# A gated-MLP block behind retention attention on one core: fewer tiles turned by TensorE, more by DMA, and a new order of the first loads

## The chip, the cores and the metric

The kernel runs on one core of a Trainium2 chip. The metric is the device time of one execution in microseconds (us); it was measured three times before the change: 209.21, 209.40 and 210.75 us, median 209.4 us.

## What is computed

Inputs are float32. q, k and v have 8 batches, 8 heads, 576 positions and 64 features. First comes attention with a decay instead of a softmax, then a block with a gate that mixes positions:

```python
scores = scale * np.matmul(q, k.transpose(0, 1, 3, 2))
ret = scores * Dmat          # Dmat[h, t, s] = gamma_h ** (t - s) for t >= s, else 0
x = matmul(ret, v)           # heads joined: (8, 576, 512)
h = gelu(x @ w_in)           # 512 -> 1024
u, v = h[..., :512], h[..., 512:]
v_n = (v - mean) / sqrt(var + 1e-6) * g_ln
v_s = einsum('ts,bsd->btd', w_sg, v_n) + b_sg[None, :, None]
out = x + (u * v_s) @ w_out
```

## The kernel before, in words

**Units and pairs.** The work is cut into 36 units (N). Two batches form a pair of 1152 rows; a pair has nine units (U = 9), and there are four pairs. A unit holds q, k and v of 256 positions for four heads (or, the fifth of a pair, the unit MID, the last 64 positions of both batches for all heads): three loads of 256 KB, for MID six of 128 KB in shorter rows. Two units that lie side by side together give two tiles of 128 rows of x.

**Attention, per unit i.** `load` (L311) issues the loads on SyncE's queue (SP). `scaled` (L504) multiplies q and v by powers of the decay (gq and gv) and turns q, k and v to bf16, on POOL for most units. Then q and k must be turned so that the 64 features lie on partitions, which makes qkT. For the first TD = 20 units TensorE (PE) turns them: eight transposes (L547) into PSUM and one copy by VectorE (DVE, L550). For the other 16 units `transposed` (L491) issues one DMA transpose for two units on SP (L499). `score` (L566) makes the products of q and k, `mask` (L577) applies the triangle, `states` (L596) makes the k-v products that carry the past into later units, `keep` (L626) adds them up on ScalarE (ACT) and DVE, and `outp` (L678) makes x, which ACT and DVE write to xT. From unit 9 on (JOIN = 8) outp of unit i-1, score of i and states of i are one visit of PE; before that they are three.

**The block, per tile of 128 rows.** `mlp_V` (L815) multiplies x by the second half of w_in (four matmuls of 512 columns, L821), and ACT, DVE and POOL make the normalised v_n. `mlp_U` (L857) multiplies by the first half (L868). `batch` (L878) does the mixing of positions (L890) and the product with w_out (L923); for the first 18 of 36 tiles x is added by four more PE transposes (L926), for the last 18 a DMA transpose of x (xr, L913) is added by DVE.

**What sets the order.** Every step is given to a planner (`Plan`, L120) with an engine, a cost, a key, its reads and writes. A table written out by hand (TURN, L19) gives each step its place in one sequence of some 1200 places; `emit` goes through it in that order and issues each step on its engine. An engine takes its steps strictly in that order. Where the planner's own clock shows PE idle in the first 45 us, `idle` (L147) puts in matmuls of zeros (L301) that feed nothing.

**Loads and weights.** There are six buffers for q and k (qkf) and six for v (vf). `lb` (L308) gives the first four units only two of them (0, 1, 1, 0), and unit MID waits for the load of unit 3. `w_load` (L338) brings w_in in four pieces of 512 KB on POOL's queue; the DMA itself turns float32 into bf16. Two pieces hold the second half (for mlp_V), two the first half (for mlp_U). The first is issued at 7.73 us, and the two of the first half wait for vb of unit 1. g_ln and b_sg are loaded with one number to a partition (`g_and_b`, L390), w_sg and w_out on SP (`weights`, L447).

Of the kernel before, what the change touches and what calls it, by code (L numbers as in the profile page):

```python
# [19 lines left out]
    "b_col": [57],  # L20
    "b_rows": [0, 58],
    "b_tr": [72],
    "dtab": [33],
# [4 lines left out]
    "g_col": [76],  # L28
    "g_col1": [89],
    "g_inv": [90],  # L30
    "g_rows": [21, 109],
    "g_tr": [121],
    "gelu": [51],
# [6 lines left out]
    "ident": [4],  # L40
# [12 lines left out]
    "otu": [48, 55, 92, 110, 136, 162, 197, 268, 304, 335, 377, 419, 447, 472, 498, 539, 554, 582, 610, 640, 673,  # L53
        703, 718, 751, 782, 823, 839, 883, 914, 946, 969, 1004, 1026, 1053, 1068, 1101],
    "out": [381, 477, 403, 384, 652, 668, 612, 790, 677, 777, 757, 788, 760, 880, 906, 932, 1069, 1070, 979, 1074,
        1082, 1132, 1135, 1115, 1105, 1094, 1124, 1144, 1150, 1146, 1158, 1174, 1178, 1184, 1183, 1188, 1190],
    "qkT": [32, 16, 44, 95, 111, 137, 170, 203, 263, 296, 334, 360, 401, 413, 421, 465, 514, 533, 550, 581, 588, 641,
        715, 754, 855, 893, 965, 1052],
    "qs": [22, 9, 40, 45, 102, 125, 154, 168, 246, 261, 267, 309, 350, 354, 386, 404, 436, 437, 487, 501, 516, 570,
        634, 639, 658, 653, 738, 696, 741, 833, 854, 843, 915, 917, 973, 937],  # L60
    "ret": [36, 35, 26, 27, 75, 69, 99, 101, 115, 116, 155, 148, 186, 194, 222, 226, 292, 279, 305, 332, 343, 363,
# [58 lines left out]
class Plan:  # L120
# [36 lines left out]
    def emit(self):  # L157
# [16 lines left out]
        for n in sorted(range(len(units)), key=lambda n: self.place[n]):  # L174
# [12 lines left out]
            if e == "PE" and t < FILL_END:  # L187
                self.idle(free[e], t)
# [18 lines left out]
def kernel(  # L207
# [757 lines left out]
    for i in range(N):  # L965
# [7 lines left out]
        if not i:  # L973
            for c in (0, 2):
                w_load(1, c)
# [41 lines left out]
```

## Time and profile before

| | us |
|---|---|
| median of three runs | 209.4 |
| the profiled execution, its time | 209.62 |
| its span (first to last instruction) | 207.9 |
| PE busy | 194.2 |
| DVE, POOL, ACT busy | 150.8, 135.8, 134.7 |
| the matmuls of zeros (L301), part of PE busy | 11.4 |

The sum of the lines on PE is the length of the span less the time in which PE has nothing. A line of the chain of waits has its start, its length and what ran; a line of the view by stretches has the stretch, the length, the busy time of each engine with its count of instructions, the clock that TensorE was granted (1.00 is full speed), the mean busy share of the 16 DMA engines (it can be over 1.00, since packets of one engine overlap) and the GB/s that they moved.

### The profile page before, as it was taken

What the parts mean: (1) busy time and instruction counts of PE and PEld (TensorE: products, weight loads), DVE (VectorE), ACT (ScalarE), POOL (GpSimd) and SP (SyncE); (2) the same over time, 40 slices, a digit from 0 to 9 for tenths busy, and PEclk for the clock granted to TensorE, in tenths of its full rate; (3) what the DMA queues carried; (4) which work ended last, traced back from release to release, by engine and by line L of the source; (5) the groups of instructions that cost most, each with busy time, mean ns of one, the idle gap of its engine ahead of it and who ended that gap; (6) DMA issues with size and microseconds to landing.
All of it is one profiled execution on the core that took longest, in us unless ns stands there. A gap on an engine that the chain in (4) does not pass through costs nothing.

```text
span 207.9 us, 7429 instructions
## 1 busy us (share of the span) xinstructions
PE 194.2 (93%) x2994; PEld 124.2 (60%) x3027; DVE 150.8 (73%) x366; ACT 134.7 (65%) x316; POOL 135.8 (65%) x231
## 2 busy tenths in 40 slices
PE   6977949999999999999999999999999999999992
PEld 2543536768767776567745666575656565664651
DVE  1654953998987888978786658575869689896672
ACT  5363325799999846788589776765777377826400
POOL 6557989489769996759779865749846866123200
PEclk9999966999999999999999999999999999999999
DMA  5999999999999998695999899998998999895815
GB/s 145 267 203 192 228 274 302 300 296 309 192 277 251 290 330 213 175 241 136 265 210 299 229 175 199 271 317 208 255 267 236 201 175 262 192 189 195 249 54 202
DMA packets 98321, 48.20 MB, mean 232 GB/s; under 512 B 42288, under 2 KB 92720, under 8 KB 98288
## 3 DMA queue, kind: packets, MB, share of 16 engines
q1 hardware_dynamic: 97056, 46.56, 90.0%
q0 software_dynamic: 1088, 1.05, 3.6%
q8 instruction: 23, 0.38, 0.8%
q10 hardware_dynamic: 144, 0.13, 0.2%
q14 instruction: 10, 0.08, 0.1%
HBM read 32.79 MB, written 9.44 MB: 203 GB/s over the span
## 4 chain that ended last, share of the span: by engine, by line
PE 85%; DMA 8%; POOL 2%; issue 2%; DVE 1%; SPq 0%; DVEq 0%; POOLq 0%
PE p_d L890 19%; PE p_d L868 16%; PE p_d L923 14%; PE p_d L821 14%; PE p_oz L692 7%; PE p_d L547 4%; DMA w_in<-in_moe_w_in_dram 4%; PE p_s L572 3%; DMA vf<-in_v_dram 3%; PE p_d L926 2%; DMA qkf<-in_q_dram 1%; PE p_oz L605 1%; PE p_d L301 1%; PE p_d L460 1%; POOL vb L537 1%
## 5 line engine op out<-in xcount | busy, mean ns | idle before, releaser
L586 DVE TENSOR_TENSOR ret<-p_s,tri 128x512 bf16<-128x512 f32 x64 | 42.5, 681 | 3.2 <-PE p_s L572 3.0
L537 POOL TENSOR_TENSOR vb<-vf,gv 128x512 bf16<-128x512 f32 x36 | 37.6, 1046 | 6.9 <-DMA vf<-in_v_dram 6.0
L890 PE MATMUL p_d<-wT,vn 128*128 128x288 bf16 x256 | 40.5, 286 | 0.0
L868 PE MATMUL p_d<-xT,w_in 128*128 128x512 bf16 (+2 forms) x224 | 37.9, 314 | 2.1 <-DMA w_in<-in_moe_w_in_dram 2.1
L534 POOL TENSOR_TENSOR qkb<-qkf,gq 128x512 bf16<-128x512 f32 x35 | 36.5, 1047 | 4.3 <-DMA qkf<-in_q_dram 2.8
L821 PE MATMUL p_d<-w_in,xT 128*128 128x512 bf16 x126 | 34.8, 380 | 1.3 <-issue 0.5
L923 PE MATMUL p_d<-w_out,uT 128*128 128x512 bf16 (+1 forms) x137 | 34.5, 373 | 0.9 <-issue 0.5
L898 DVE TENSOR_TENSOR uT<-p_d,uT 128x288 bf16<-128x288 f32 x64 | 27.6, 448 | 6.1 <-PE p_d L890 4.8
L890 PEld LDWEIGHTS <-vn 128*128 128x128 bf16 x256 | 24.4, 98 | 7.1
L873 ACT ACTIVATE uT<-p_d 128x512 bf16<-128x512 f32 x36 | 21.2, 596 | 11.1 <-PE p_d L868 11.0
L853 ACT ACTIVATE vn<-vg,stat 128x512 bf16<-128x512 f32 x32 | 25.6, 814 | 3.8 <-POOL stat L840 3.7
L868 PEld LDWEIGHTS <-w_in 128*128 128x128 bf16 x224 | 19.4, 101 | 13.6 <-DMA w_in<-in_moe_w_in_dram 2.3
L838 POOL TENSOR_TENSOR stat<-stat,mhalf 128x1 f32<-128x1 f32 x36 | 20.2, 562 | 11.0 <-DVE stat L832 6.0
L824 ACT ACTIVATE vg<-p_d 128x512 f32<-128x512 f32 x36 | 20.9, 596 | 9.3 <-PE p_d L821 9.2
L829 DVE BATCH_NORM_STATS2 stat<-vg 128x6 f32<-128x512 f32 x36 | 24.6, 684 | 2.5 <-ACT vg L824 2.4
L530 POOL CAST qkb<-qkf 128x512 bf16<-128x512 f32 x32 | 19.5, 613 | 8.5 <-DMA qkf<-in_k_dram 5.8
L550 DVE COPY qkT<-p_d 128x1024 bf16<-128x1024 bf16 x20 | 13.7, 683 | 11.7 <-PE p_d L547 11.5
L923 PEld LDWEIGHTS <-uT 128*128 128x128 bf16 x148 | 13.7, 98 | 13.1
L821 PEld LDWEIGHTS <-xT 128*128 128x128 bf16 x144 | 13.0, 98 | 12.2 <-DVE xT L772 0.4
L837 POOL TENSOR_SCALAR stat<-stat 128x1 f32<-128x1 f32 x26 | 5.6, 217 | 20.7 <-DVE stat L830 15.6
L890 PE MATMUL p_d<-wT,vmid 128*128 128x288 bf16 x64 | 18.4, 287 | 0.0
L547 PE MATMUL p_d<-ident,qkb 128*128 128x128 bf16 x160 | 13.3, 229 | 1.0 <-POOL qkb L534 0.8
(103 smaller groups left out, 308.3 us busy)
## 6 DMA issues: line engine op xcount, KB each, us to landing
out_dram<-ob SPq DMA_DIRECT2D x35, 256.0 KB, 3.9
qkf<-in_q_dram SPq DMA_DIRECT2D x32, 256.0 KB, 5.4
qkf<-in_k_dram SPq DMA_DIRECT2D x32, 256.0 KB, 5.5
vf<-in_v_dram SPq DMA_DIRECT2D x32, 256.0 KB, 5.6
wsg<-in_moe_w_sg_dram SPq DMA_DIRECT2D x4, 288.0 KB, 5.1
w_in<-in_moe_w_in_dram POOLq DMA_DIRECT2D x4, 256.0 KB, 5.7
qkf<-in_k_dram SPq DMA_DIRECT2D x8, 128.0 KB, 5.1
qkf<-in_q_dram SPq DMA_DIRECT2D x8, 128.0 KB, 5.0
```

The costliest lines, as they stand in the source:

```text
L534: plan.add("POOL" if i else "DVE", 1010 if i else 700, key, lambda: eng.tensor_tensor(split(qs[a]), shape(qkf[l][:, 0, :]), gain(gq), op=A ...
L537: plan.add("POOL", 1010, key + 2, lambda: nc.gpsimd.tensor_tensor(shape(vb[a][:]), shape(vf[l][:]), gain(gv), op=Alu.mult), reads=rd(i, 2) ...
L547: nc.tensor.transpose(banks[0][:].bitcast(BF)[:, (x * KK + kk) * 128:(x * KK + kk + 1) * 128], src[:, kk * 128:(kk + 1) * 128], ident[:])
L586: nc.vector.tensor_tensor(ret[r][x][:].rearrange("p (s k j) -> p s k j", s=2, k=2), banks[0][:].rearrange("p (s k) j -> p s k j", s=2), tr ...
L821: nc.tensor.matmul(banks[0][:], xT[p % NX][:, m, kk, :], w_in[:, kk, F2:], start=(kk == 0), stop=(kk == KK - 1))
L829: nc.vector.bn_stats(st[:, 0:6], vg[g][:])
L853: nc.scalar.activation(vn[p % 2][m][:], vg[g][:], Act.Identity, scale=st[:, 8:9], bias=st[:, 9:10])
L868: nc.tensor.matmul(hu[:, c, :].rearrange("p (t j) -> p t j", j=128), w_in[:, kk, 128 * (x * per + c):128 * (x * per + c) + 128], xT[p % NX ...
L873: plan.add("ACT", 500, key, lambda banks, x=x: nc.scalar.activation(uT[p % NX][:, x * per:x * per + per, cols], banks[0][:].rearrange("p ( ...
L890: nc.tensor.matmul(banks[0][:, :HS], src[:, 128 * c:128 * c + 128], wT[e][j][:, half * HS:(half + 1) * HS], start=(j == 0), stop=(j == SB ...
L898: plan.add("DVE", 380, key, lambda banks, c=c, col=col: nc.vector.tensor_tensor(uT[x][:, c, col:col + HS], banks[0][:, :HS], uT[x][:, c, c ...
L923: nc.tensor.matmul(banks[0][:, :w], uT[x][:, c, r], w_out[:, c, x0:x0 + w], start=(c == 0), stop=late and c == KK - 1, skip_group_check=True)
```

## The change

Six things change together, and the table TURN is new throughout.

1. TD goes from 20 to 16: the units 16 to 19 are turned by two more DMA transposes on SP, so ten in place of eight.
2. JOIN goes from 8 to 6: units 7 and 8 are also visited in one piece.
3. `lb` gives unit i the buffer i mod 6, so each of the first six units has its own, and the wait of unit MID for the load of unit 3 is gone.
4. `w_load` loads w_in as float32 on SP, in four pieces of 256 columns, into the buffers of the output (ob) and one new buffer (wst). ACT turns the two pieces of the second half to bf16, POOL those of the first. mlp_V of the first two tiles is cut in two halves of 256 columns, each waiting for its own piece; mlp_U waits only for the piece that it needs.
5. g_ln and b_sg are loaded as nine rows (gb); one PE transpose and one DVE copy make the columns.
6. Some steps may run on one of two engines; a second table (SIDE) says on which. Eight of the loads are issued on ACT's queue. `idle` puts in zeros up to 350 ns past the planned idle time where the planner's clock is under 32 us.

```diff
-    JOIN, TD = 8, 20
+    JOIN, TD = 6, 16
...
-                self.idle(free[e], t)
+                self.idle(free[e], t + (350 if t < 32000 else 0))
...
+    wst = sb("wst", [128, KK, F2 // 2], F32)
...
     def lb(i):
-        return (0, 1, 1, 0)[i] if i < 4 else (i - 2) % NL
+        return i % NL
...
-                             reads=[("ld", 0, lb(3), 0)] if i == MID else [], writes=[("ld", a, l, e)], dma=600)
+                             writes=[("ld", a, l, e)], dma=550)
...
     def w_load(half, c):
-        plan.add("POOL", 770, (1 - half) * T0 + 10 + c, lambda: nc.gpsimd.dma_start(
-            w_in[:, c:c + 2, half * F2:(half + 1) * F2],
-            moe_w_in.rearrange("(c p) f -> p c f", p=128)[:, c:c + 2, half * F2:(half + 1) * F2]),
-            reads=[("ld", 1, 0, 0)] if half else [("vb", 1)], writes=[("w_in", half, c), ("w_in", half, c + 1)], dma=1500)
+        x = 2 * (1 - half) + c
+        part_ = wst[:] if x == 3 else obs[x][:].rearrange("p a f -> p (a f)").rearrange("p (k f) -> p k f", k=KK)
+        held = [] if x == 3 else [("ob", 2 * x), ("ob", 2 * x + 1)]
+        f0 = half * F2 + c * (F2 // 2)
+        plan.add("SP", 560, (1 - half) * T0 + 10 + c, lambda: nc.sync.dma_start(
+            part_, moe_w_in.rearrange("(k p) f -> p k f", p=128)[:, :, f0:f0 + F2 // 2]),
+            writes=[("wf", x)] + held, dma=1420)
+        plan.add({"ACT": 965, "POOL": 985}, None, (1 - half) * T0 + 10 + c, lambda e: copy(
+            e, w_in[:, :, f0:f0 + F2 // 2], part_),
+            reads=[("wf", x)] + held, writes=[("w_in", half, c)])
...
-        plan.add("SP", 600, -1.1 * T0, lambda: nc.sync.dma_start(
-            g_col[:], moe_g_ln.rearrange("(c p) -> p c", p=128)), reads=[("ld", 0, lb(2), 0)], writes=["g_col"], dma=300)
+        full = S // 128
+        plan.add("SP", 500, -1.1 * T0, lambda: nc.sync.dma_start(
+            gb[:KK, :], moe_g_ln.rearrange("(c p) -> c p", p=128)), reads=["dtab"], writes=[("gb", 0)], dma=100)
...
+        u = plan.add("PE", 230, 2 * T0, lambda banks: nc.tensor.transpose(banks[0][:, :KK + SB], gb[:], identf[:]),
+                     reads=[("gb", 0), ("gb", 1), "identf"], writes=["gb_tr"], take=[("d", 1)])
...
-        def mm(banks):
-            for kk in range(KK):
-                nc.tensor.matmul(banks[0][:], xT[p % NX][:, m, kk, :], w_in[:, kk, F2:],
-                                 start=(kk == 0), stop=(kk == KK - 1))
+        parts = 2 if i < 2 else 1
+        w = F2 // parts
+        for y in range(parts):
+            def mm(banks, y=y):
+                for kk in range(KK):
+                    nc.tensor.matmul(banks[0][:, y * w:y * w + w], xT[p % NX][:, m, kk, :], w_in[:, kk, F2 + y * w:F2 + y * w + w],
+                                     start=(kk == 0), stop=(kk == KK - 1), skip_group_check=parts > 1)
```

**SyncE's queue around the loads of w_in.** The rows are issues in their order; qkf0 to qkf5 and vf0 to vf5 are the six buffers, ob0 to ob2 and wst the places where the pieces of w_in now land. Before, this queue had no w_in; from its 13th issue on stood

```order
L319 DMA qkf2_63<-in_k_dram 64x8x64
L327 DMA vf0_67<-in_v_dram 128x4x128
L327 DMA qkf0_61<-in_k_dram 128x4x128
L391 DMA g_col_152<-in_moe_g_ln_dram 128x4x1
L319 DMA qkf2_63<-in_q_dram 64x8x64
...
L319 DMA vf2_69<-in_v_dram 64x8x64 x2
L327 DMA qkf3_64<-in_q_dram 128x4x128
L327 DMA qkf3_64<-in_k_dram 128x4x128
L327 DMA vf3_70<-in_v_dram 128x4x128
```

and now, from its 15th issue on:

```order
L367 DMA vf2_69<-in_v_dram 128x4x128
L383 DMA ob0_144<-in_moe_w_in_dram 128x4x256
L367 DMA vf3_70<-in_v_dram 128x4x128
L383 DMA ob1_145<-in_moe_w_in_dram 128x4x256
L359 DMA qkf4_65<-in_k_dram 64x8x64
L359 DMA qkf4_65<-in_q_dram 64x8x64
...
L359 DMA vf4_71<-in_v_dram 64x8x64 x2
L367 DMA qkf5_66<-in_k_dram 128x4x128
L383 DMA ob2_146<-in_moe_w_in_dram 128x4x256
L383 DMA wst_147<-in_moe_w_in_dram 128x4x256
L367 DMA qkf0_61<-in_k_dram 128x4x128
```

The four pieces of w_in now stand between the loads of units 2 to 5, and the loads of unit 6 come behind the last.

**POOL's queue around the first half of w_in.** vb and qkb are the scaled v, q and k. Before:

```order
L537 TENSOR_TENSOR vb2_77<-vf1_68,gv_165 128x512
L339 DMA w_in_147<-in_moe_w_in_dram 128x2x512
L537 TENSOR_TENSOR vb3_78<-vf0_67,gv_165 128x512
L672 CAST zsA0_95<-s2_1_94 128x128
...
L404 TENSOR_TENSOR g_col_152<-g_col_152,g_tmp_153 128x4
L339 DMA w_in_147<-in_moe_w_in_dram 128x2x512
L534 TENSOR_TENSOR qkb0_73<-qkf2_63,gq_164 128x4x2x64
```

Now:

```order
L577 TENSOR_TENSOR vb1_76<-vf5_72,gv_167 128x512
L878 TENSOR_TENSOR stat0_118<-stat0_118,mhalf_168 128x1
L343 CAST w_in_148<-ob2_146 128x4x256
L343 CAST zsA0_95<-zmid0_89 128x256
L343 CAST w_in_148<-wst_147 128x4x256
L343 CAST qkb1_74<-qkf0_61 128x2x4x64
```

Two issues of DMAs left this queue, and two casts of 1024 numbers to a partition came in, behind the scaling of unit 5's v and ahead of unit 6's k.

**PE around the first product with the first half of w_in.** Before, the first of these (L868) stood behind outp of unit 3 and score and states of unit 4 (the eight matmuls into each of the two targets are one row here), and the transposes of unit 5 came after it:

```order
L692 MATMUL p_oz_169<-ret3_1_88,vb3_78 64x128
...
L572 MATMUL p_s1_168<-qkT0_79 64x64
...
L605 MATMUL p_d2_172<-vb0_75,qkb0_73 64x64
...
L868 MATMUL p_d1_171<-xT0_99,w_in_147 128x256
...
L547 MATMUL p_d0_170<-ident_159,qkb0_73 128x128
```

Now the same product is L908:

```order
L587 MATMUL p_d2_174<-ident_161,qkb0_73 128x128
...
L857 MATMUL p_d3_175<-w_in_148,xT0_99 128x512
...
L725 MATMUL p_oz_171<-ret0_1_82,vb0_75 64x64
...
L612 MATMUL p_s0_169<-qkT0_79 64x128
...
L645 MATMUL p_d2_174<-vb1_76,qkb0_73 64x64
...
L908 MATMUL p_d1_173<-xT0_99,w_in_148 128x256
```

Ahead of it there now stand also the transposes, score and states of unit 5, outp of unit 4 and the product with the second half of w_in (L857) for a third tile.

More of the change, by code (lines that the diff above doesn't have):

```diff
@@ L57 @@
[L57 to L61, printed above, removed]
[8 rows of a table removed]
-    "srow": [2],
-    "srow_i": [1],
[5 rows of a table removed]
@@ new lines @@
+SIDE = {
+    "kb": "PAAPAPPAPPAPPPPAAAAPAPPPAPPAPPAAPPPA",
+    "ld": "SSSSSSSSSSSSSASSSSSSAASSSSSSSSSSSSSSSSSSSSSSSSSSSSSSSSSSSSSSSSSSSSSSSSSSSSSSSSSSSSSSSSSSSSSSSSSSSSSSSSSSSSSSSSAAASASSSSA",
+    "out": "SSSSSSSSSSSSSSSSSSSSSSSSSSSSSSSSSSSAS",
+    "qkT": "DAAADADADDDDADDA",
+    "qs": "DDPDPPPPPDPPPPDDPPPDPPPPPPPPPPPPDPPP",
+    "vb": "PPPDPPDPPPPPPPPPPDPDPPPPPPDPPPPPPPPD",
+    "wT": "DDDDD",
+    "wT1": "APPPA",
+    "w_in": "AAPP",
+    "wnat": "PPPPA",
+    "zbdA": "PPAPPAAAAPAPPPPPPAAPAPPAPAPP",
+    "zbdB": "--PPAAPA--PAAPPP--AAPAPA--AAAPPP",
@@ L141, in add @@
         mine = self.seen[name] = self.seen.get(name, -1) + 1
+        if isinstance(engine, dict):
+            sides, some = engine, emit
+            self.sides[len(self.units)] = sides
+            engine = self.side[name][mine] if name in self.side else next(iter(sides))
+            engine = {e[0]: e for e in sides}[engine[0]]
+            cost, emit = sides[engine], lambda *banks: some(engine, *banks)
         self.look[len(self.units)] = look
@@ L303, with copy @@
     xr_turn = [0]
-    plan = Plan({"s": p_s, "oz": [p_oz], "d": p_d}, TURN, fill)
+    plan = Plan({"s": p_s, "oz": [p_oz], "d": p_d}, TURN, SIDE, fill)
+    by = {"POOL": nc.gpsimd, "DVE": nc.vector}
+    queue = {"SP": nc.sync, "ACT": nc.scalar}
+    def copy(e, dst, src):
+        if e == "ACT":
+            nc.scalar.activation(dst, src, Act.Copy)
+        else:
+            by[e].tensor_copy(dst, src)
     T0 = 5300.0
@@ L939, in batch @@
                 last = i == NP * NT - 1 and not x0
-                queue = nc.scalar if last else nc.sync
-                plan.add("ACT" if last else "SP", 400, key, lambda i=i, o=o, x0=x0, w=w, queue=queue: queue.dma_start(
+                plan.add({"ACT": 450} if last else {"SP": 450}, None, key, lambda g, i=i, o=o, x0=x0, w=w: queue[g].dma_start(
                     outf[128 * i:128 * i + 128, x0:x0 + w], ob[o][:, :w]),
-                    reads=[("ob", o)], writes=[("out", i, x0)], dma=720 * w // DM)
+                    reads=[("ob", o)], writes=[("out", i, x0)], dma=650 * w // DM)
     def done(i):
@@ L973 @@
         if not i:
-            for c in (0, 2):
+            for c in range(2):
                 w_load(1, c)
@@ L980 @@
         if i == 1:
-            for c in (0, 2):
+            for c in range(2):
                 w_load(0, c)
```

222 lines of the change are left out of this document (113 added, 109 removed), and 109 rows, old and new, of the table TURN.

## The prediction

> **What bounds the kernel now.** I read the slices of the page first, then who waited for whom on PE, then the chain of waits and the stretches of time.
>
> ```profile
> PE   6977949999999999999999999999999999999992
> PEclk9999966999999999999999999999999999999999
> DMA  5999999999999998695999899998998999895815
> ```
>
> A slice is 5.2 us. From the eighth (36 us) on PE is full to the last but one. Before that it has gaps, and its clock is low in the sixth and seventh slice. DMA is full nearly everywhere.
>
> Who waited on PE, first over the whole span, then (second fence) from 34 us on, where these two rows are all:
>
> ```profile
> PE p_d L868 <- DMA w_in<-in_moe_w_in_dram: 2.1, 1, 2.1
> PE p_d L605 <- POOL vb L537: 2.0, 2, 1.4
> ```
>
> ```profile
> PE p_d L923 <- issue: 0.5, 3, 0.2
> PE p_d L821 <- issue: 0.5, 3, 0.2
> ```
>
> From 34 us on PE waits for nothing but its own issue, 1.0 us in all. So there are two ways to gain: less work for PE, and more of it done before 34 us. The chain of waits (start, length, what) shows what sets that moment:
>
> ```profile
> 21.84 7.45 DMA w_in<-in_moe_w_in_dram
> 29.33 3.60 PE p_d L868 x16
> 32.92 0.85 PE p_d L547 x8
> 33.78 0.47 PE p_oz L692 x16
> ...
> 36.76 0.45 PE p_d L547 x8
> 38.91 0.98 PE p_d L868 x8
> 41.20 0.46 PE p_oz L692 x24
> 42.63 0.35 PE p_s L572 x16
> 43.10 0.98 PE p_d L868 x8
> 58.82 0.40 PE p_oz L692 x20
> 85.20 0.86 PE p_d L821 x4
> 110.39 0.46 PE p_oz L692 x24
> 111.20 0.32 PE p_d L821
> ```
>
> The last piece of w_in is issued at 21.84 us behind POOL's other work and lands at 29.29; the first product with it starts at 29.33. Its first 16 matmuls take 3.60 us, eight like them later take 0.98: half speed. The stretches around it say why (the last three columns are granted clock, DMA share, GB/s):
>
> ```profile
> 27.40:27.60 0.20, 0.00 (x0) 0.00 (x0) 0.20 (x1) 0.00 (x0) 0.20 (x2) 0.99 0.93 251
> 27.60:27.80 0.20, 0.00 (x0) 0.00 (x0) 0.17 (x2) 0.00 (x0) 0.20 (x2) 0.50 1.08 279
> 34.20:34.40 0.20, 0.20 (x5) 0.11 (x2) 0.20 (x1) 0.10 (x1) 0.20 (x1) 0.50 1.07 338
> 34.40:34.60 0.20, 0.20 (x1) 0.09 (x1) 0.20 (x2) 0.20 (x2) 0.20 (x1) 0.94 1.29 355
> ```
>
> While PE waits for w_in its clock falls to 0.50 at 27.6 us, and is back at 34.4 us, 5.1 us after work began again.
>
> The Trainium skill (TensorE: Matmul & The Clock Gate, section "What's actually happening") has the clock fall after at least one window of about 3.4 us without work. Here it fell inside a wait of 2.1 us, so the trace is stricter than that rule. By the rule, a shorter wait would cost only its length, my first rival below would fall away, and the sum would stay as it is.
>
> **The start, worked out.** When can the first product with the first half of w_in start in the changed kernel? It needs the third piece of w_in. Ahead of that and with it DMA must move units 0 to 3 and 5 and q of unit 6 (16 loads of 0.262 MB, 4.19 MB), unit 4 in shorter rows (0.79 MB), and three pieces of w_in (1.57 MB): 6.55 MB.
>
> ```profile
> 10.00:20.00 10.00, 7.30 (x135) 3.96 (x136) 4.44 (x12) 4.51 (x12) 6.24 (x10) 1.00 1.03 196
> 20.00:30.00 10.00, 6.86 (x137) 4.03 (x136) 8.31 (x24) 3.47 (x9) 8.63 (x20) 0.88 1.12 242
> 30.00:40.00 10.00, 9.95 (x178) 7.45 (x178) 5.21 (x14) 6.26 (x15) 6.81 (x10) 0.78 1.09 299
> ```
>
> The DMA queues in the first two of these stretches (packets, MB, share of 16 engines), 10 to 20 us and 20 to 30 us:
>
> ```profile
> q0 software_dynamic: 526, 0.51, 32.3%
> ```
>
> ```profile
> q0 software_dynamic: 544, 0.52, 38.0%
> ```
>
> DMA is full in all three, but moves 196 and 242 GB/s while the casting queue of w_in takes a third of the engines for 0.5 MB, and 299 once it is done. The change takes that queue away, so I price at 299: 4.19 MB are 14.0 us, w_in 5.3 us. The rows of unit 4 are half as long; between 299 and 196 GB/s they take 2.6 to 4.0 us, I take 3.3, the middle. Together 22.6 us.
>
> ```profile
> 0.79 0.45 SPq L327 DMA_DIRECT2D qkf<-in_q_dram  x1
> 4.06 1.04 POOL L534 TENSOR_TENSOR qkb<-qkf,gq 128x512 bf16<-128x512 f32 x1 [0.70 <-DMA qkf<-in_q_dram]
> ```
>
> ```profile
> L530 POOL CAST qkb<-qkf 128x512 bf16<-128x512 f32 x32 | 19.5, 613 | 8.5 <-DMA qkf<-in_k_dram 5.8
> ```
>
> A load of 0.88 us of data issued at 0.79 is used at 4.06 us, so 2.4 us are a head and a tail. I put both, with the 0.8 us from last byte to use, at 3.2 us: the piece lands at 25.8. POOL's cast of 1024 numbers is two of 613 ns, 1.2 us. So PE starts that product at **27.0 us** in place of 29.33: **-2.3**. Bounds: from 1.25 us on PE has, by my count along its order, some 13 us of useful work and 42 matmuls of zeros ahead of it (before, 37 of them are 11.4 us of busy time that partly overlaps the work behind; I take 11 us), so not before 25.4 (-3.9); at 242 GB/s it is 31.5 us (+2.2).
>
> **What is already done by then.** The order on PE puts ahead of it, beside what stood there before, the transposes of unit 5 (0.45), outp of unit 4 (0.40), score and states of unit 5 (42.63 to 43.10: 0.47) and a third tile of mlp_V (0.86): **-2.2**. This is work of PE that fills what were gaps. If its loads are late it stays in the path: 0 to -2.2.
>
> **The clock.** If it stays at 1.00, the 16 matmuls cost 2 x 0.98 for 3.60 (-1.64), the transposes 0.45 for 0.85 (-0.40), and 33.78 to 34.4 half (-0.3): **-2.4**, at most half of 5.1 us. More zeros stand around this place now, which speaks for it. If the wait comes all the same, 0.
>
> **Less work.** Four units less are turned by PE, 4 x 0.45: **-1.8**. Their copies on DVE (L550) go too; DVE is no bound (15.59 us busy of 19 in the stretch where these units lie, quoted below), so nothing. Two visits joined: apart, outp 0.46 and score with states 0.47 are 0.93; joined, 110.39 to 111.20 is 0.81: **-0.2**. The one transpose of g and b, and the two halves of mlp_V, lie among zeros: nothing; uncovered some 0.3 us.
>
> **What is late next.** After 27 us PE goes on faster than the loads were planned for. Behind the last piece of w_in (27.6 us) come five loads (4.4 us) and w_sg (1.33 MB, 4.4 us), landing at 36.4, 37.1 with POOL's cast. PE's work from 27.0 to the turning of w_sg is 10.1 us by the rows above: 37.1. Then unit 9's q lands at 40.8, scaled and cast at 42.5, and PE wants it at 42.6. Both fit without slack, so I add **+1.0** for what slips; 0 to +4.
>
> The two more DMA transposes stand on SP in the stretch from 77 to 96 us:
>
> ```profile
> 36.00:77.00 41.00, 40.37 (x743) 29.98 (x750) 36.29 (x94) 36.16 (x77) 33.49 (x46) 1.00 1.09 279
> 77.00:96.00 19.00, 18.58 (x364) 12.34 (x358) 15.59 (x37) 14.30 (x33) 13.39 (x23) 1.00 0.82 217
> 96.00:168.00 72.00, 71.31 (x1143) 44.86 (x1145) 51.48 (x125) 49.85 (x121) 51.52 (x85) 1.00 0.95 233
> ```
>
> ```profile
> L499 SPq DMA_TRANSPOSE qkT<-qkb x8: 2331/2976/3700, 96.4 to 167.9; - x8
> ```
>
> ```profile
> SPq L499 <- POOL stat L840: 11.9, 4, 3.5
> ```
>
> Each holds SP for 2.98 us, and SP also waits ahead of it for POOL (four times, 11.9 us in all, with loads and outputs queued behind). From 96 to 168 us seven or eight of them are done at a share of 0.95 with PE full (71.31 of 72). From 77 to 96 the share is 0.82, so there is room for two: nothing. Without that cover they cost up to 2 x 3 us of loads.
>
> **The sum:** -2.3 -2.2 -2.4 -1.8 -0.2 +1.0 = -7.9, from 209.6 (the profiled execution: span 207.9 and 1.7 around it, which stay) to 201.7. The median was 0.2 below that execution: **201.5 us**.
>
> **The rivals.**
>
> *The clock falls again.* The third piece is late by a us or two, the zeros run out, and PE is at half speed as before. For it: 2.1 us sufficed. Against: more zeros. It loses the 2.4: 203.9 us. 0.17.
>
> *DMA becomes the bound.*
>
> ```profile
> q1 hardware_dynamic: 97056, 46.56, 90.0%
> q0 software_dynamic: 1088, 1.05, 3.6%
> ```
>
> These two shares and 1.1% of the rest are 94.7% of 207.9, 196.9 us of all 16 engines. Less 7.5 for the old w_in (3.6%), plus 7.0 for the new (2.1 MB at 299), plus two transposes at no more than their 3.0 each: 202.4. My span of 199.8 needs a mean share of 1.01. For it: that is more than 0.95. Against: 1.09 over 41 us. If 1.00 is the most, 202.4 and 1.7 is 204.1 us. 0.13.
>
> *Stalls eat the lead.* Engines keep strictly to an order that is new everywhere; late loads cost 6 us more after 27 us: 207.5, within 1%. 0.03.
>
> *Slower: the first loads stay at the rate of 10 to 20 us.* The cast leaves DMA, so twice the bytes are written for w_in, all behind each other on SP. At 196 GB/s 6.55 MB take 33.4 us, the product starts at 37.8 (+8.5), the clock falls, and with -2.2, -1.8 and -0.2 it is 213.7 us. It decides from some 225 GB/s down. Against: the low rate goes with the casting queue, which is gone. 0.05.
>
> **How the numbers follow.** The forecast has 0.62. About 1% (2.1 us) is what a measurement of this kernel can tell from no change. Faster by over 1%: 0.62 + 0.17 + 0.13 = 0.92; within: 0.03; slower: 0.05. Range: the earliest start (-1.6 more) and no slip (-1.0) with a little on the clock give 198.5; the first rival with 2 us more of slip gives 205.8.
>
> **What would show it.** Right: the first product with the first half of w_in starts near 27 us; the clock stays 1.00 from 20 to 35 us; its first 16 matmuls take 2.0 us; 128 transposes on PE in place of 160; PE has no wait over 1 us after 45 us; its work ends near 196 us. Wrong: that product after 29 us, a clock of 0.50 past 25 us, waits of PE for POOL or DMA between 36 and 100 us, or a GB/s under 240 before 26 us.

## The result: 3.4% slower

The changed kernel takes 217.0 us (median of four runs, 215.5 to 217.8) against 209.5 us of the kernel before beside it: a ratio of **1.034, 95% interval 1.027 to 1.041**. The forecast was 201.5 us. The granted clock of TensorE differs between executions of one and the same kernel and the time goes with it, so each ratio below leaves the disturbed executions out and can differ a little from that of the medians. The profiled execution after took 217.77 us, with a span of 215.9 (before 209.62 and 207.9).

### The profile page after: what moved, and what is told of

Read it like the earlier page. It is cut to its first block, busy times and chain, and to the rows that moved or that the text cites. A ratio compares the mean times of both kernels' runs of the same rounds, so it can differ in the third digit from the quotient of the medians.

```text
span 215.9 us, 7441 instructions
## 1 busy us (share of the span) xinstructions
PE 193.4 (90%) x2975; PEld 122.1 (57%) x3010; DVE 155.9 (72%) x372; ACT 137.9 (64%) x308; POOL 128.5 (60%) x231
## 4 chain that ended last, share of the span: by engine, by line
PE 38%; DMA 20%; SPq 14%; DVE 11%; POOL 8%; issue 4%; ACT 3%; DVEq 0%; POOLq 0%; ACTq 0%
PE p_d L930 13%; PE p_d L963 6%; PE p_d L857 6%; DMA qkf<-in_q_dram 5%; PE p_d L908 5%; SPq L367 5%; DMA qkT<-qkb 4%; SPq L359 4%; DMA ob<-in_moe_w_in_dram 3%; PE p_oz L725 3%; DMA xr<-xT 3%; POOL vb L577 3%; DVE qkb L574 3%; DVE ret L626 2%; DMA out_dram<-ob 2%
## 5 line engine op out<-in xcount | busy, mean ns | idle before, releaser
L574 POOL TENSOR_TENSOR qkb<-qkf,gq 128x512 bf16<-128x512 f32 x28 | 29.6, 1059 | 15.4 <-DMA qkf<-in_q_dram 15.0
L577 POOL TENSOR_TENSOR vb<-vf,gv 128x512 bf16<-128x512 f32 x30 | 32.1, 1073 | 9.9 <-DMA vf<-in_v_dram 8.9
L908 PE MATMUL p_d<-xT,w_in 128*128 128x512 bf16 (+2 forms) x224 | 36.0, 303 | 0.0
L857 PE MATMUL p_d<-w_in,xT 128*128 128x512 bf16 (+1 forms) x135 | 34.8, 367 | 1.2 <-issue 0.5
L864 ACT ACTIVATE vg<-p_d 128x512 f32<-128x512 f32 x36 | 21.5, 597 | 11.7 <-PE p_d L857 10.8
L908 PEld LDWEIGHTS <-w_in 128*128 128x128 bf16 x224 | 18.3, 98 | 10.1
L963 PEld LDWEIGHTS <-uT 128*128 128x128 bf16 x148 | 13.9, 98 | 17.0 <-issue 4.4
L857 PEld LDWEIGHTS <-xT 128*128 128x128 bf16 x152 | 13.9, 98 | 13.1 <-issue 1.7
L973 DVE TENSOR_TENSOR ob<-p_d,xr 128x512 f32<-128x512 f32 (+1 forms) x19 | 12.3, 657 | 9.0 <-PE p_d L963 4.1
L930 PE MATMUL p_d<-wT,vmid 128*128 128x288 bf16 x64 | 18.3, 287 | 0.2 <-DVE qkT L343 0.2
L343 POOL CAST qkb<-qkf 128x512 bf16<-128x512 f32 x21 | 12.7, 610 | 7.3 <-DMA qkf<-in_k_dram 7.3
L332 PE MATMUL p_d<-zero 128*128 128x512 bf16 x38 | 13.9, 456 | 3.2 <-ACT vg L864 1.6
L612 PE MATMUL p_s<-qkT 64*64 64x128 bf16 (+1 forms) x576 | 14.3, 218 | 2.5 <-DMA qkT<-qkb 2.5
```

Of the source, the lines that this page charges most:

```text
L574: plan.add({"POOL": 1000, "DVE": 620}, None, key, lambda e: by[e].tensor_tensor(split(qs[a]), shape(qkf[l][:, 0, :]), gain(gq), op=Alu.mul ...
L577: plan.add({"POOL": 1000, "DVE": 620}, None, key + 2, lambda e: by[e].tensor_tensor(shape(vb[a][:]), shape(vf[l][:]), gain(gv), op=Alu.mul ...
L857: nc.tensor.matmul(banks[0][:, y * w:y * w + w], xT[p % NX][:, m, kk, :], w_in[:, kk, F2 + y * w:F2 + y * w + w], start=(kk == 0), stop=(k ...
L864: plan.add("ACT", 500, key, lambda banks: nc.scalar.activation(vg[g][:], banks[0][:], Act.Gelu_apprx_tanh), reads=[("hv", i), ("hw", i)], ...
L908: nc.tensor.matmul(hu[:, c, :].rearrange("p (t j) -> p t j", j=128), w_in[:, kk, 128 * (x * per + c):128 * (x * per + c) + 128], xT[p % NX ...
L930: nc.tensor.matmul(banks[0][:, :HS], src[:, 128 * c:128 * c + 128], wT[e][j][:, half * HS:(half + 1) * HS], start=(j == 0), stop=(j == SB ...
```

## The profile after

The slices of the page (5.4 us each), as shown of the kernel before:

```profile
PE   7947969987999999999979799999759999999993
PEclk9996999999999999999999999999999999999999
DMA  5999899999999997899999999999999999984346
```

The gaps of PE before 36 us are still there; new are those in the slices 9, 10, 21, 23, 29 and 30 (43 to 54, 108 to 124 and 151 to 162 us). The clock falls in the fourth slice now, not in the sixth and seventh. DMA, which had a 6 around 86 us and a 5 around 96 us, has an 8 and a 9 there. Who waited on PE (total, times, longest); these are all rows over 1 us:

```profile
PE p_oz L725 <- ACT zsB L341: 2.8, 1, 2.8
PE p_s L612 <- DMA qkT<-qkb: 2.5, 2, 1.4
PE p_d L963 <- DVE ob L973: 2.1, 1, 2.1
PE p_d L587 <- DVE qkb L574: 1.8, 2, 1.5
PE p_d L332 <- ACT vg L864: 1.6, 1, 1.6
PE p_d L587 <- POOL qkb L574: 1.3, 2, 1.1
PE p_d L332 <- DVE zero L1001: 1.2, 1, 1.2
PE p_d L963 <- ACT uT L913: 1.1, 1, 1.1
```

No row names w_in any more. ACT's copies, DMA transposes (qkT), scaled tiles (qkb) and tiles to be put out (ob) stand there in its place. The stretches of the prediction (columns as there):

```profile
10.00:20.00 10.00, 6.06 (x132) 3.56 (x132) 3.97 (x8) 4.74 (x14) 5.70 (x11) 0.91 1.13 274
20.00:30.00 10.00, 8.50 (x166) 5.67 (x169) 5.69 (x15) 4.28 (x9) 4.31 (x8) 0.91 0.97 246
30.00:40.00 10.00, 9.27 (x175) 6.28 (x176) 9.02 (x25) 8.28 (x20) 9.17 (x13) 1.00 1.09 303
36.00:77.00 41.00, 38.17 (x695) 27.88 (x699) 37.34 (x90) 33.30 (x72) 33.65 (x43) 1.00 1.07 265
77.00:96.00 19.00, 18.68 (x318) 11.92 (x320) 14.91 (x37) 16.16 (x33) 14.07 (x27) 1.00 1.04 218
96.00:168.00 72.00, 65.42 (x1068) 40.57 (x1079) 49.63 (x119) 44.79 (x105) 46.46 (x83) 1.00 1.15 247
```

The first loads do flow faster: 274 GB/s from 10 to 20 us, where it was 196. But from 96 to 168 us PE is busy 65.42 us, where it was 71.31, at a DMA share of 1.15, where it was 0.95.

**Where the time went.** PE's span is useful work, matmuls of zeros and idle time. From the busy time of PE by stretches, with and without the line of the zeros (us):

| profiled run | span | useful | zeros | idle to 36 us | idle after 36 us |
|---|---|---|---|---|---|
| before | 207.9 | 182.8 | 11.4 | 7.6 | 6.1 |
| after | 215.9 | 179.5 | 13.9 | 8.3 | 14.3 |
| after, all loads on SyncE (e1) | 213.1 | 179.9 | 12.8 | 6.3 | 14.1 |
| e1 with less to load (e6) | 206.9 | 179.9 | 14.3 | 6.0 | 6.8 |
| new start, old order (e9) | 207.0 | 179.3 | 14.5 | 6.1 | 7.1 |

Useful time fell by 3.3 us, of the 4.2 that fewer transposes and a clock that stays up were to give. The zeros took 2.5 more, the start gave nothing back, and after 36 us PE stands 8.2 us longer: -3.3 +2.5 +0.7 +8.2 is 8.1, the 8.0 between the spans.

## Experiments on the start

**ACT stands still behind its own loads.** In the order of the program each DMA issue on SyncE's and ACT's queue waits for the landing of the DMA eight issues earlier, counted over both: the v of unit 2 landed at 16.23 us and ACT's first load was issued at 16.25, the third piece of w_in landed at 28.77 and ACT's third load was issued at 28.79. Eight loads are issued by ACT now. ACT's timeline around the first three (the last number in brackets is the idle time ahead):

```profile
16.25 0.71 ACTq L359 DMA_DIRECT2D qkf<-in_q_dram  x1
17.01 0.28 ACT L341 ACTIVATE zsB<-p_d 128x128 bf16<-128x128 f32 x1 [4.40 <-DMA vf<-in_v_dram]
...
22.53 0.41 ACTq L367 DMA_DIRECT2D vf<-in_v_dram  x1
22.99 1.06 ACT L341 ACTIVATE w_in<-ob 128x1024 bf16<-128x1024 f32 x1 [2.12 <-DMA qkf<-in_q_dram]
...
28.79 0.38 ACTq L367 DMA_DIRECT2D qkf<-in_q_dram  x1
29.27 0.38 ACT L785 ACTIVATE xs<-p_oz 128x256 f32<-128x256 f32 x1 [3.60 <-PE p_d L587]
```

Before each issue ACT stands 2 to 4.4 us, the copies that PE wants queued behind. The second load (v of unit 5) is itself late, and POOL with it: its vb waits 1.76 us for that load at 29.38, and the cast of w_in's third piece stands behind that vb, to 30.90 us. So on PE:

```profile
17.34 0.25 PE L725 MATMUL p_oz<-qkT,zsB 64*64 64x128 bf16 x4 [2.79 <-ACT zsB L341]
...
30.50 0.38 PE L332 MATMUL p_d<-zero 128*128 128x512 bf16 x1 [1.57 <-ACT vg L864]
...
32.58 1.58 PE L908 MATMUL p_d<-xT,w_in 128*128 128x256 bf16 x13
```

The product with the first half of w_in starts at 32.58 us, not at 27.0 and not even at the old 29.33. The first of these runs moves the eight loads to SyncE:

```diff
-    "ld": "SSSSSSSSSSSSSASSSSSSAASS...SAAASASSSSA",
+    "ld": "SSSSSSSSSSSSSSSSSSSSSSSS...SSSSSSSSSSS",
```

> The changed kernel with all loads issued by SyncE, none by ACT. Three theories of the 7.5 us by which the change is slower than before (217.0 against 209.5). A, ACT stands still: a load issued by ACT waits in ACT's own queue until the load eight issues earlier has landed, and so holds the copies behind it (ACT waited 4.4 us for a load at 16.25 us and 3.6 us up to 29.27). By A this kernel gains at least 4 us: 213 or less, the first product with the first half of w_in starts before 31 us, and the clock stays at 1.00 from 18 to 22 us. B, the two more DMA transposes and a full DMA from 77 us on: nothing or under 1 us, 216 to 217.5. C, w_in as float32 at the start: the first product stays near 32.6 us and the time near 217, since the loads on SP now only wait for one another in another queue.

Measured: 214.5 us (212.6 to 215.8), ratio 1.026 (1.019 to 1.034). In the profiled execution the product starts at 29.76 us, the clock is 1.00 throughout, ACT's two long waits are gone, and the span is 2.8 us shorter. So A holds for the start. In time it is 2.5 us by the medians, less than the 4 that I gave it, and as the intervals of the two ratios overlap, even that gain is not certain. Idle time after 36 us is as long as before it (14.1 us), so the larger part of the loss is elsewhere.

**Own buffers, zeros and the clock.** Three runs put parts of the start into the kernel before. The first has `return i % NL` in `lb` and unit MID's wait removed; the second has eight zeros ahead of the product that waits for w_in; the third has the change's rule for zeros alone.

```diff
+                for _ in range(8 if (p, ms[0], x) == (0, 0, 1) else 0):
+                    fill(banks[0])
```

```diff
-                self.idle(free[e], t)
+                self.idle(free[e], t + (350 if t < 32000 else 0))
```

> The kernel before with one part of the change alone: each of the first six units has its own buffers, and unit MID no longer waits for the load of unit 3. If the loads wait for buffers at the start, they come earlier and the kernel gains 0 to 1 us. If more loads in the air only delay the casting transfers of w_in, whose last piece sets the start of the block (29.33 us), it loses 0.5 to 3 us.

> The kernel before with one thing added: eight matmuls of zeros (1.7 us at full clock) ahead of the first product with the first half of w_in, into its own bank, where PE waits 2.1 us for w_in and its clock falls to 0.50 until 34.4 us. If the clock is what the wait costs beside its length, as the prediction's third term has it (2.4 us): 206.5 to 208 against 209.2 in the same call, and the 16 matmuls behind take 2.0 us in place of 3.6. If the lost half speed is made up elsewhere (loads come no earlier): no difference over 0.5 us.

> The kernel before with one part of the change alone: matmuls of zeros up to 350 ns past the planned idle time where the planner's clock is under 32 us, 62 of them in place of 37. If they fill only time in which PE would have stood: 207 to 209, with the clock at 1.00 through the wait for w_in. If zeros that nobody waits out push the work behind them: up to 25 x 0.22 = 5.4 us more in the worst case, 210 to 213.

Measured: 209.9 us, ratio 0.998 (0.983 to 1.013); 208.2 us, ratio 1.001 (0.996 to 1.006); 207.8 us, ratio 1.000 (0.993 to 1.006). None tells itself from the kernel before. The second did not test what it was to test: in its profiled execution the clock had fallen to 0.50 at 29.48 us, just before the zeros, seven of them took 3.19 us, and the product started at 32.67 us. The third does what was wanted. Its stretches up to, in and after the wait for w_in:

```profile
20.00:27.40 7.40, 7.15 (x138) 3.99 (x138) 6.61 (x18) 3.22 (x8) 6.56 (x15) 1.00 1.11 206
27.40:28.70 1.30, 0.46 (x11) 0.30 (x7) 1.27 (x5) 0.38 (x1) 1.30 (x3) 1.00 1.13 317
28.70:36.00 7.30, 7.25 (x169) 5.64 (x171) 5.09 (x13) 5.42 (x13) 6.50 (x10) 1.00 1.13 304
```

The clock stays at 1.00 and the profiled span is 205.3 us, 2.6 less than that of the profiled execution before. Yet the ratio says no gain. That does not price the clock itself: over all executions of that call the mean clock was 0.996 or more in nine of ten with the rule and in three of 23 without it, and the medians are 207.8 and 209.4 us. So a gain through the clock is neither shown nor excluded; its loss was common in the kernel before, but not the same in every execution.

## Experiments on what comes after 36 us

**The transposes.** TD alone, first put back in the changed kernel (units 16 to 19 turned by PE), then both edits so far together, then changed alone in the kernel before:

```diff
-    JOIN, TD = 6, 16
+    JOIN, TD = 6, 20
```

```diff
-    JOIN, TD = 8, 20
+    JOIN, TD = 8, 16
```

> The changed kernel with units 16 to 19 turned by TensorE again, so eight DMA transposes instead of ten, the first from 96 us on. B says that the stalls of PE at 108 and 118 us (1.1 and 1.4 us) shrink and the loads behind SP come earlier: 1.8 us more of PE, 3 to 5 us less of stalls, 213 to 216. A and C say that the work of PE comes on top: 217 to 219.

> Both of the edits before: all loads on SyncE, and units 16 to 19 turned by TensorE. If A and B both hold, the gains add: 209 to 212. If A alone holds, this is slower by up to 1.8 us than the kernel with the loads on SyncE alone. If C holds, 217 or more.

> The kernel before with TD = 16 and nothing else: the four units 16 to 19 turned by two more DMA transposes. My prediction had 1.8 us less on PE and nothing for the transposes: 207.7. B says that SP, held by two more transposes and by the scaled tiles that they wait for, brings loads late: 209.5 to 213. A and C say that this part is not what costs: 207.5 to 209.

Measured: 216.7 us, ratio 1.039 (1.033 to 1.044); 216.3 us, 1.030 (1.021 to 1.039); and 216.0 us, 1.032 (1.023 to 1.041). In the kernel before, this one edit costs as much as the whole change, and PE waits for the transposes themselves:

```profile
PE p_s L572 <- DMA qkT<-qkb: 6.8, 2, 3.7
```

(The two places at which the new transposes stand in that table are mine; other places may cost less.) In the changed kernel taking the edit back gains nothing that can be told: the waits for qkT go, 1.8 us of transposes come back on PE, and other waits take the place. The 209 to 212 us that both edits together were to give by A and B did not come. So the transposes are dear in the kernel before, and they are not the whole cause in the changed one.

What they cost shows in the DMA queues. First the kernel before with TD = 16, then the changed kernel with all loads on SyncE with 16 units turned by PE, then with 20, last again with 16 (the run e5 of a later section, whose DMA work is the same as that of the second):

```profile
q1 hardware_dynamic: 101216, 47.61, 92.4%
q0 software_dynamic: 1088, 1.05, 3.7%
```

```profile
q1 hardware_dynamic: 102210, 49.71, 98.6%
```

```profile
q1 hardware_dynamic: 98050, 48.66, 93.6%
```

```profile
q1 hardware_dynamic: 102210, 49.71, 96.7%
```

With 1.0% of small queues the first is 97.1% of 213.9 us, 207.7 us of all 16 engines, against 196.9 before: 10.8 us for two transposes. The second is 99.6% of 213.1, 212.2 us; the third 94.7% of 213.4, 202.1 us: 10.1 us for two. But the last is 97.8% of 211.3, 206.7 us, 5.5 less than the second for the same work, and the work of the kernel before took 196.9 to 201.1 us in four profiles (before, e7, e15, e16). So two transposes add some 8 to 11 us of packet time, and single profiles do not fix it. The packet records of the traces tell what it is made of: two transposes are 4096 more packets of 256 bytes. At the mean that packets of this size had in these runs (25 to 28 ns) that is 6.4 to 7.1 us, **3.2 to 3.6 us of all 16 engines for one**, near the 3.0 that I had taken from the time that the issue holds SyncE. The rest is that other packets of 256 bytes took longer: half of all took 18 ns or less, single ones up to 2.4 us.

**How full the DMA is.** One run takes load off the changed kernel with all loads on SyncE, one puts load on the kernel before:

```diff
-                             dst[:].rearrange("p (h f) -> p h f", h=HU),
-                             src[2 * p + e, c * HU:c * HU + HU, r0:r0 + 256, :]...
+                             dst[:].rearrange("p (h f) -> p h f", h=HU)[:, :hs],
+                             src[2 * p + e, c * HU:c * HU + hs, r0:r0 + 256, :]...
```

```diff
+                             for to in ([dst, spare[i % 2]] if more else [dst])],
```

> The changed kernel with all loads on SyncE, and from unit 20 on the loads (but for those of the units MID) bring only half of their data, 5.5 MB of 50 less; this leaves part of the input out. B, a full DMA is what stalls PE from 100 us on (1.5 and 2.0 us in the longest two waits, about 4 us more idle than before in 100 to 180 us): the stalls go and the time falls by 3 us or more, to 211.5 or less. If the stalls come from the order in which engines take their steps, it falls by less than 1 us: 213.5 to 214.5.

> The kernel before, whose order is kept, with a fuller DMA: from unit 20 on each load of v (but for the units MID) is issued twice, the second time into a buffer that nobody reads, 3.7 MB more in 14 issues on SyncE. B, the fullness of the DMA alone costs what the change lost (its DMA rows sum to 212.9 us of 16 engines with all loads on SyncE, against 196.9 before; here 196.9 and some 14): 211 to 216, with waits of PE for loads after 130 us. If the order of before has the slack to carry it, and it is the new order that lacks it: 208.5 to 210.

Measured: 209.7 us (e6), ratio 1.004 (0.997 to 1.012), 4.8 us less than with full loads; and 221.5 us (e14), ratio 1.050 (1.034 to 1.067), 11.6 us more by the medians and 10.5 by the ratio than the kernel before. The stretch from 100 to 180 us, with all loads on SyncE, then with the late ones halved:

```profile
100.00:180.00 80.00, 75.21 (x1222) 45.97 (x1235) 57.46 (x138) 53.41 (x123) 50.55 (x94) 1.00 1.11 241
```

```profile
100.00:180.00 80.00, 80.00 (x1302) 48.44 (x1296) 61.80 (x146) 56.77 (x130) 52.19 (x99) 1.00 0.85 200
```

At a share of 0.85 PE is never idle there, with the new order, the new engines and ten transposes all in place. And the kernel before, its DMA filled to 96.4% of 222.0 us, starts to wait where it never did:

```profile
PE p_s L574 <- DMA qkT<-qkb: 7.9, 4, 2.7
```

So B holds, in both directions: the kernel before lies close under what its DMA can deliver in time, and the change goes over it. (Of the 11.6 us not all is fullness: SyncE also waited 7.2 us for a spare buffer to land before it could be used again, and the profiled execution ran at a mean clock of 0.969.)

**The order.** The next runs join the new start (all loads on SyncE, 20 units by PE) to the old order from one place in the table on; the mend of the first is in the choice of engines:

```diff
-    "zbdA": "PPAPPAAAAPAPPPPPPAAPAPPAPAPP",
+    "zbdA": "PPAPPAAAAAAAAAAAAAAAAAAAAAAA",
```

> The changed kernel up to its place 230 (some 36 us; all loads on SyncE, 20 units turned by TensorE), and from there on the order and the engines of the kernel before. Theory E, the new start is worth 3 us and the new order after it costs more than that: PE has no wait over 1 us after 45 us, and the time is 205 to 207. If the lead of the start cannot be kept because loads come late for any order, 208 to 210. If the start is no better than before, 209 or more.

> The graft of the run before (the changed kernel up to place 230, all loads on SyncE, then the order of the kernel before), with one mend: there the carries of the past into later units (zsA, zsB) had stayed on POOL, and PE waited 5.9 us at 153 us for one that stood behind POOL's other steps; now ACT makes them, as in the kernel before. Theory E (the new start is worth 3 us, the new order after it costs it): 206 to 208, and no wait of PE over 1.5 us after 45 us. Theory B for any order (the DMA is too full with w_in as float32): 209 or more with waits of PE for loads.

> The same graft with the seam at place 258 (some 40 us) in place of 230, so that the sum of unit 6 is not torn apart at the seam, where PE waited 1.2 us in the graft before. Theory E: 205 to 207.5. Theory B: 209 or more.

Measured: 216.6 us (e8), ratio 1.038 (1.031 to 1.046); then, mended, 209.7 us (e9), 1.007 (1.002 to 1.013); and 210.9 us, 1.010 (1.005 to 1.014). The first lost 7 us against the second, to one wait of PE and the lower clock behind it (0.6 in two slices):

```profile
PE p_oz L755 <- DVE xT L835: 5.9, 1, 5.9
```

which goes back to DVE:

```profile
DVE s L734 <- POOL zsA L373: 7.6, 2, 7.0
```

A carry of 0.3 us stood on POOL behind its other steps, scaled tiles above all. Mended, PE has no wait after 60 us but its own issue:

```profile
PE p_d L993 <- issue: 0.5, 3, 0.2
PE p_d L887 <- issue: 0.3, 2, 0.2
```

That graft moves the bytes of the run "both" (49.3 MB) and is 6.4 us shorter in its profile (207.0 against 213.4), so at equal bytes the new order, with its choice of engines, costs about 6 us. But theory E also said that the new start is worth 3 us, and that falls: the grafts are 0.7 and 1.0% behind the kernel before, not ahead of it.

**Engines or places?** Two runs keep the new places and give the old engines back, all of them (20 units by PE) or the carries only (16):

> The changed kernel's own order throughout, with all loads on SyncE and 20 units turned by TensorE (216.3 us in an earlier run), but from place 230 on each step that has a choice of engine goes where the kernel before has it: q, k and v are scaled on POOL alone, the carries zsA and zsB and the copies of the second w_sg are made by ACT. Theory F, the new choice of engines is what costs (POOL stands at carries that wait for DVE, DVE is locked out by POOL): 208 to 211. Theory E in its narrow form, the new places in the table cost: 213 to 217, since the places are those of the change.

> The changed kernel with all loads on SyncE (214.5 us in an earlier run), and from place 230 on the carries zsA and zsB on ACT, as in the kernel before, in place of 24 of them on POOL or ACT by the new table; q and v scaled as in the change. Theory F narrowed to the carries: POOL stood 12.3 us at zsB for DVE, so the scaled tiles and with them SyncE's transposes and loads come earlier: 210 to 212.5. If ACT, which now has them, is late for others, or if the carries on POOL cost nothing there: 213.5 to 217.

Measured: 223.5 us, ratio 1.077 (1.069 to 1.085), and 215.5 us, 1.037 (1.026 to 1.048). Theory F falls: new places and new engines belong together, and the places cost more without them.

**Single waits.** After 45 us the longest wait of PE with all loads on SyncE is one of 2.7 us for a scaled tile from DVE. DVE and POOL there:

```profile
45.56 1.04 POOL L577 TENSOR_TENSOR vb<-vf,gv 128x512 bf16<-128x512 f32 x1
...
45.76 3.63 DVE L574 TENSOR_TENSOR qkb<-qkf,gq 128x512 bf16<-128x512 f32 x1
46.55 0.28 POOL L343 CAST zsB<-s 128x128 bf16<-128x128 f32 x1
46.80 1.04 POOL L577 TENSOR_TENSOR vb<-vf,gv 128x512 bf16<-128x512 f32 x1
47.80 1.03 POOL L574 TENSOR_TENSOR qkb<-qkf,gq 128x512 bf16<-128x512 f32 x1
48.90 1.49 POOL L343 COPY wT<-wT 64x1152 bf16<-64x1152 bf16 x1
49.31 0.68 DVE L343 COPY qkT<-p_d 128x1024 bf16<-128x1024 bf16 x1
```

DVE's product of two tiles takes 3.63 us, where the same instruction mostly takes 0.69; it ends half a microsecond after the last of POOL's four instructions that began behind each other. The next two runs move it to POOL, then also move two transposes of x ahead:

```diff
-    "qs": [12, 25, 65, 77, 104, 75, 171, 180, 221, 279, ...
+    "qs": [12, 25, 65, 77, 104, 75, 171, 180, 221, 252.5, ...
-    "qs": "DDPDPPPPPDPPPPDDPPPDPPPPPPPPPPPPDPPP",
+    "qs": "DDPDPPPPPPPPPPDDPPPDPPPPPPPPPPPPDPPP",
```

```diff
-    "xr": [850, 877, 964, ...
+    "xr": [819.5, 820.5, 964, ...
```

> The changed kernel with all loads on SyncE, and one step moved: the scaling of unit 9's q goes from DVE to POOL, ahead of the scaling of unit 8's v. In the run with all loads on SyncE that step took 3.63 us on DVE (0.69 elsewhere) while POOL ran three products of two tiles in SBUF one after the other, and PE waited 2.7 us for it. Theory D, DVE is locked out by POOL: the step takes 1.04 us on POOL, the wait of PE shrinks under 0.5 us, and the time falls by 2 us or more below that run (214.5). If the wait is made up later anyway, since late loads bound the middle, 214 to 215.

> The changed kernel with all loads on SyncE, with the two longest waits of PE after 45 us mended where they arise: unit 9's q scaled by POOL ahead of unit 8's v (PE waited 2.7 us for it on DVE), and the first two DMA transposes of x (xr) moved up from places 850 and 877 to 820 (PE waited 2.0 us at 153.7 us for the tile that DVE adds them to). If the loss after 36 us sits in such single waits: 214.5 less 2.5 to 4.5 us, 210 to 212. If each wait that is taken away comes back at the next late load, as with the first of them alone (213.9): 213 to 215.

Measured: 213.9 us, ratio 1.023 (1.014 to 1.032); and 218.6 us, 1.042 (1.030 to 1.053). The first takes the wait away (PE's idle time from 36 to 60 us falls from 3.95 to 1.35 us) and the median falls by 0.6: new waits of 1.3 and 1.0 us come at 90 and 115 us, and that at 152 us stays. The second is no better and probably worse; PE now waits (in a profiled execution with a mean clock of 0.969)

```profile
PE p_s L612 <- DMA qkT<-qkb: 4.3, 1, 4.3
PE p_oz L725 <- POOL zsB L343: 2.3, 1, 2.3
```

So taking single waits away did not win the loss back: new ones came at other places.

**Both remedies.** Last, the new order with 20 units by PE and the late loads halved:

> The changed kernel with all loads on SyncE and 20 units turned by TensorE (216.3 us), with the late loads halved from unit 20 on as in the run e6 (this leaves part of the input out). Same DMA work as the graft of the new start and the old order up to there (209.6), which has no waits after 60 us. If the new order loses its time to loads that come late in a full DMA: 207.5 to 210, no waits of PE over 0.5 us after 100 us. If the new places themselves stall PE: 212 or more.

Measured: 215.2 us, ratio 1.027 (1.009 to 1.046), 1.1 us less than with full loads, which cannot be told from nothing. PE is idle 2.4 us from 60 to 180 us, so the late waits go here too. But 4.6 us of idle time lie between 36 and 60 us, 3.5 of them behind the same locked-out product on DVE. So a full DMA alone does not explain the time of this kernel. Why it stays so far above e6 (209.7 us) is partly told by the 1.8 us of transposes and by the clock, which fell behind that wait (0.93 from 36 to 60 us); the wait itself e6 has too (2.5 us). The rest stays open, as does which of the new places cost most. No run was faster than the kernel before by more than its interval.

## Why the prediction was wrong, step by step

**"So PE starts that product at 27.0 us": wrong, 32.58.** The rate (274 and 246 GB/s up to 30 us) is under the 299 that I priced, but the rival of slow first loads did not come. What failed is to price the loads as one stream of 22.6 us with 3.2 for head and tail: issues wait for the landing of the eighth before them, the third piece was issued only at 22.01 us, and the loads given to ACT held ACT, and through a late v also POOL. With all loads on SyncE it is 29.76 or, in the run with both edits, 27.84 us, so the estimate was near for a kernel without that part. (Each is one profiled execution.) I had listed the eight loads among the changes and priced them at nothing.

**"What is already done by then": -2.2 predicted, and the work is there.** Up to that product stand 48 transposes for 40, 96 matmuls of score for 80 and three tiles of mlp_V for two. PE's busy time without the zeros grew by less, from 10.4 to 11.2 us; that is rough, since zeros and work overlap in it. As the product itself came 3.25 us later, no lead came of it.

**"If it stays at 1.00", -2.4: half right.** The 16 matmuls behind the start now take 1.91 us, as forecast. (The three parts of this term add up to 2.34, not 2.4.) But the clock falls earlier, behind the 2.8 us wait for zsB:

```profile
18.00:19.00 1.00, 1.00 (x25) 0.80 (x23) 0.00 (x0) 1.00 (x5) 0.34 (x1) 0.65 1.31 170
19.00:20.00 1.00, 1.00 (x14) 0.19 (x6) 0.95 (x2) 1.00 (x3) 0.00 (x0) 0.50 1.35 170
20.00:21.00 1.00, 1.00 (x18) 0.46 (x19) 0.37 (x3) 0.87 (x1) 0.00 (x0) 0.50 1.21 148
21.00:22.00 1.00, 0.78 (x3) 0.27 (x2) 1.00 (x2) 0.00 (x0) 0.29 (x1) 0.65 0.72 88
```

Much of what runs there is zeros, so this execution lost little by it. And the term was not the same in every execution of the kernel before: the profiled one had 6.83 us at half clock, others a mean clock of 1.00 (see the last section).

**"Less work, -1.8 and -0.2": about right for the transposes**; the row of L547 and L587 went from 13.3 us for 160 to 10.0 for 128, the slow clock of before included. The joined visits were not tried alone.

**"From 77 to 96 the share is 0.82, so there is room for two: nothing": wrong.** This is the step that failed most plainly: in the kernel before, these two transposes alone, at the places that I gave them, cost 3.2%, as much as the whole change, with 6.8 us of waits for them on PE. In the changed kernel the share of that stretch went from 0.82 to 1.04, and in the 72 us behind it from 0.95 to 1.15. The price of 3.0 us for a transpose was near what its own packets take (3.2 to 3.6); what I had wrong is the room. I took the free share of a mean for free time at the moment at which it is wanted, and counted nothing for the packets that slow each other down.

**"+1.0 for what slips; 0 to +4": wrong, +8.2** of idle time after 36 us. "Both fit without slack" was the warning, and I gave it one microsecond. Two causes are shown: the full DMA (4.8 us when it is relieved) and the new order with its engines (6 us at equal bytes in the kernel with 20 units by PE). They overlap and cannot be added. The lock-out of DVE held PE for 1.5 us here and 2.7 with the loads on SyncE, but taking it away gained nothing that can be told.

**The rival "DMA becomes the bound" was the nearest in mechanism, at too low a price.** It made 202.4 us of all engines and 204.1 in all. Four profiles with its work (ten transposes, w_in as float32, all loads on SyncE: e1, e5, e13 and the run with the carries on ACT) have 206.7 to 216.0 us of packet time, 98 to 100% of their spans. Yet packet time is no fixed cost: it moves with the waiting in the queues, and the run with both edits has 202.1 us of it in a time of 216.3 us. So a full DMA is part of the loss and does not give the time by itself. The only rival on the slower side, slow first loads (213.7 us), had the direction right by a mechanism that did not come.

## What to carry to other kernels

Where PE and DMA are both over 90% busy, an exchange that takes work off one must be priced on both, in what it does to the queues of the other and not by the mean share that is free there; two DMA transposes saved PE 1.8 us, added 8 to 11 us of packet time to the DMA engines and made the kernel before 3.2% slower. A DMA issued from a computing engine's queue is an instruction of that engine: when an issue can wait for an earlier landing, all copies behind it wait too. In an order written out by hand, a wait that was taken away here was followed by new ones elsewhere, and new places cost more without the engines that they were made for; so such an order is to be changed and measured as a whole.

## What the runs showed of the hardware that I had not expected

- A product of two tiles on DVE (128x512, both operands in SBUF) took 3.08 to 3.63 us in place of 0.69 while POOL ran one instruction with SBUF operands after the other. The Trainium skill (SBUF — State Buffer, section "Who interferes with whom") has such a DVE instruction contend with a GpSimd one that reads SBUF, the second to issue blocked until the first is done. The trace agrees that it blocks, and shows more: with all loads on SyncE it was not let in between POOL's instructions, but ended 0.56 us behind the fourth (48.83 and 49.39 us).
- A DMA transpose of 128 x 2048 bf16 is 2048 packets of 256 bytes. At their median of 18 ns they would be 2.3 us of all 16 DMA engines; at the mean, which a few long packets lift to 25 to 28 ns where transposes were added or taken back, 3.2 to 3.6 us. Its landing grows with the load: 5.3 us (median) before, 7.9 us after.
- One kernel does not lose its clock to the same extent in every execution, and it loses it in steps. Between the start and the end of the traces of this case the clock stands at 0.50 for 3.41 us or a whole multiple of it (before 6.83 us from 27.6 us on, after 3.41 us from 18.3 us on; up to 10.24 us in the run with the engines of before). In 70 executions of the kernel before, the 14 with a mean granted clock of 0.996 or more took 207.3 us on the mean, 35 at 0.988 to 0.992 took 209.1, 17 at 0.980 to 0.984 took 211.0, and four at 0.972 to 0.975 took 213.5. The one with the profile had 0.984 and 209.6. So the time goes up by about 2 us with each such step, though the wait that brings the step may be part of that.
